# Attention's step loop with the normalisation behind two reductions, the splits of v one step on, their sums two steps behind, and early work placed anew

## The chip, the cores and the metric

The kernel runs on one core of one Trainium2 chip. The metric is the device time of one execution in microseconds (us). TensorE is called PE, and its weight loads, which run beside its matmuls, PEld; VectorE is DVE, ScalarE is ACT, GpSimd is POOL, and SyncE, on which nearly all DMAs are issued, is SP.

## The reference

Three stages follow each other. The first is attention over 2 batches of 8 heads, 768 rows of 64 each, with a mask: a score counts only where the signs of six random projections of q and of k are the same.

```python
mask = q_bucket[:, :, :, None] == k_bucket[:, :, None, :]
scores = np.where(mask, scale * np.matmul(q, k.transpose(0, 1, 3, 2)), -1e9)
scores = scores - np.max(scores, axis=-1, keepdims=True)
attn = np.exp(scores)
attn = attn / (np.sum(attn, axis=-1, keepdims=True) + 1e-09)
x = np.matmul(attn, v)                    # 16 heads -> x [1536, 512]
logits = x @ w_gate + modality_bias[modality_id]   # 8 experts, argmax, softmax weight
out[mask] = gate_w[mask, None] * (np.maximum(x[mask] @ w1[e], 0.0) @ w2[e])   # 512 -> 1024 -> 512
h = out @ w_in                            # 512 -> 2048
result = (np.maximum(h, 0.0) + alpha * np.minimum(h, 0.0)) @ w_out
```

The second sends each row of x to the one expert with the largest logit; the third is a feed-forward net over all rows.

## The kernel before, in words

The change lies in attention alone, so only that stage is told. Its work is written as one loop over steps, `for s in range(96+LAG+2)`. A step handles one sixth of a head (128 of its 768 keys); head h has the steps 6h to 6h+5. No loop runs on the chip: the program is written out, and each engine has one queue, in the order in which the loop writes. What stands in a step is set by `ORDER`, a word in which each letter stands for one kind of work, and by the table `PLAN`, which says in which step the work goes that comes once per head or once per group of heads.

The kinds of work of a step, with their lines:

- **ST** (letters a and b, halves of 384 queries): two matmuls (L861, L862) give the scores in a PSUM buffer `st`, ACT takes the exponential (L863). The first matmul holds the mask's bits and the row maximum as extra rows of the tile `op`, so it waits for the DMA that puts the row maximum there (`op<-mr`, L838).
- **MAX** (m and n, the same halves): a matmul on the mask's bits (L829) into `mxp`, reduced by DVE to a row maximum (L830, 0.55 us). A unit is one sixth of a head; units run some steps ahead of ST. `PLAN["cap"]` lists how many units a step takes, and behind the list's end it is two; but no unit is taken further than ten steps ahead, so that the steady rate is one. `st` and `mxp` share five PSUM buffers.
- **POSTa, POSTb** at the end of a head's MAX: a reduction (L832), a transpose on PE (L835), two short DVE instructions (L837, L841), and the DMAs of the row (L838) and of flags (L842) on SP.
- **EL** (e): the exponential is split into two halves of 16 bits, Eh on ACT (L867) and El on POOL (L868; on DVE from step 87 on).
- **AV** (A, in odd steps, for two sixths at a time, `LAG`=4 steps behind ST): 36 matmuls (L876 to L878) into the one PSUM buffer `av`. With a head's last sixth come the six L882.
- **NORM** (N, in steps 6h+10): three DVE instructions (L888, L889, L890) read `av` and write a head's part of x. The next head's AV, in the step behind, overwrites `av` and so waits for L890. For heads 7 and 15 NORM also issues the DMA of x (L892), on SP.
- **vsplit** of head h: ACT scales v into a PSUM buffer of the tag `misc` (L755, letter V), DVE splits it into `vh` (L759) and `vl` (L760, letter o). **vtot**: twelve small matmuls (L766, L767) sum them, and DVE keeps the sum in `vt` (L768, L769), which L882 reads. `misc` has two buffers, shared with Z, POSTb and the router.
- **Z**: six matmuls for a head's bits (L802 to L804, three for each half), DVE thresholds them (L809), and two DMAs on SP put them into the tile `op` (L650, `op<-big`), which MAX reads.
- **Router**: transposes of x on PE (L182) with a copy on DVE (L185), logits (L196, L200), and from step 57 a chain of small DVE instructions, cut into pieces; `PLAN["first"]` lists the steps of the pieces, the ninth being the gate weights.

In a step behind the steps of the start, the order of the letters in `ORDER` is: ST's first half (a), ACT's part of vsplit (V), the DMAs kept from before (D), NORM (N), MAX's first half (m), ST's second half (b), MAX's second half (n), EL (e), then POSTa, DVE's part of vsplit, AV and the rest.

Of the kernel before, what the change touches and what calls it, by code (L numbers as in the profile page):

```python
# [34 lines left out]
PB = 1  # L35
LAGS = (0, 0)
HB = 3
ORDER = "aVDNmbnefopAL"
PM = 2
PLAN = dict(  # L40
    v0=(1, 3, 4), T3=(2, 2), Z3=(4, 5), T=(2, 4, 5, 7), Z=(8, 10), ld=0, am1=(4, 6, 8, 9), am=(4, 6, 8,
    10), sc=(13, 15), tot=3, tot0=6, sp=(-2, 4, 10, 18), cap=(3, 2, 0, 1), x=(1, 2, 7, 3), x3=(0, 1, 2, 2), x4=(9, 10, 13, 11), w1=(91, 92, 95, 96, 97, 98, 99, 100), ga=(87, 88, 90), vl=1, am0=(0, 0), Z2=(0, 1), x6=(0, 1, 6, 4), first=(57, 58, 59, 60, 66, 72, 75, 78, 83, 84, 85, 86),
)
NPRE = 3
NT = 22
# [458 lines left out]
def _program(base, tc, nc, q, k, v, proj, mod, w_gate, mbias, w1, w2, win, wout, alpha, out):  # L504
# [445 lines left out]
    for s in range(96+LAG+2):  # L950
        us=[u for u in range(nu,min(96,s+6+LA+1,nu+(PLAN["cap"][s] if s<len(PLAN["cap"]) else 2)))]; nu+=len(us)
        fs=dq[:]; dq.clear()
        for o in "aVDNbmnefopAL" if s==0 else ORDER:
            t=s-1-LAG
# [613 lines left out]
```

## Time and profile before

| what | us |
|---|---|
| median of 3 executions | 685.57 (683.86 to 687.6) |
| the profiled execution | 686.88 |
| its span, first to last instruction | 685.1 |
| PE busy | 656.4 |
| PEld busy | 556.2 |
| DVE busy | 446.7 |
| ACT busy | 315.3 |
| POOL busy | 236.0 |

The span is what the trace covers; 1.8 us of the profiled execution lie around it. Busy time is the sum of the times in which an engine executes. Attention takes the first 250 us or so, and PE is the busiest engine in it and behind it.

### The profile page before, as it was taken

What the parts mean: (1) busy time and instruction counts of PE and PEld (TensorE: products, weight loads), DVE (VectorE), ACT (ScalarE), POOL (GpSimd) and SP (SyncE); (2) the same over time, 40 slices, a digit from 0 to 9 for tenths busy, and PEclk for the clock granted to TensorE, in tenths of its full rate; (3) what the DMA queues carried; (4) which work ended last, traced back from release to release, by engine and by line L of the source; (5) the groups of instructions that cost most, each with busy time, mean ns of one, the idle gap of its engine ahead of it and who ended that gap; (6) DMA issues with size and microseconds to landing.
All of it is one profiled execution on the core that took longest, in us unless ns stands there. A gap on an engine that the chain in (4) does not pass through costs nothing.

```text
span 685.1 us, 12778 instructions
## 1 busy us (share of the span) xinstructions
PE 656.4 (96%) x4938; PEld 556.2 (81%) x4938; DVE 446.7 (65%) x927; ACT 315.3 (46%) x536; POOL 236.0 (34%) x211
## 2 busy tenths in 40 slices
PE   7789999999999988999999999999999999999995
PEld 6578898998788878898888987888888888888884
DVE  6887878788888778455735668999443444433332
ACT  5567788887787843033423256665211111111111
POOL 8767999987967501310000202040030000200002
PEclk9979999999999999999999999999999999999998
DMA  8466864866603139385320834441020000100001
GB/s 217 129 146 142 187 154 97 185 185 138 140 11 125 49 107 395 119 321 201 108 61 11 285 120 154 131 146 62 1 93 1 15 16 0 47 16 0 1 0 61
DMA packets 32859, 75.02 MB, mean 110 GB/s; under 512 B 7276, under 2 KB 7366, under 8 KB 32534
## 3 DMA queue, kind: packets, MB, share of 16 engines
q1 hardware_dynamic: 29700, 64.43, 33.0%
q0 software_dynamic: 2960, 9.70, 4.3%
q8 instruction: 39, 0.64, 0.4%
q14 instruction: 30, 0.25, 0.1%
q10 hardware_dynamic: 130, 0.00, 0.0%
HBM read 49.79 MB, written 14.68 MB: 94 GB/s over the span
## 4 chain that ended last, share of the span: by engine, by line
PE 54%; DVE 1%; ACT 1%; issue 1%; POOL 1%; ACTq 0%; POOLq 0%
PE o L1413 19%; PE h L1387 18%; PE y L1074 8%; PE g L1054 8%; PE tr L1257 1%; POOL out_dram L1430 1%; PE tr L1041 0%; DVE w L1232 0%; DVE op L1232 0%; ACT op L1230 0%; DVE gl L620 0%; ACT gf L1391 0%; ACT q L1392 0%; ACT w L1230 0%; DVE big L1197 0%
## 5 line engine op out<-in xcount | busy, mean ns | idle before, releaser
L868 POOL TENSOR_TENSOR El<-E,Eh 128x768 f16<-128x768 f32 x87 | 142.7, 1652 | 36.6 <-ACT Eh L867 22.7
L863 ACT ACTIVATE E<-st 128x384 f32<-128x384 f32 x192 | 89.2, 494 | 53.3 <-PE st L862 49.8
L830 DVE TENSOR_REDUCE mx<-mxp 128x1 f32<-128x384 f32 x192 | 97.6, 548 | 9.2 <-PE mxp L829 8.7
L617 ACT ACTIVATE gh<-gf 128x512 fp32r<-128x512 f32 x48 | 30.3, 631 | 142.7 <-PE o L1413 132.2
L867 ACT ACTIVATE Eh<-E 128x768 f16<-128x768 f32 x94 | 79.8, 849 | 0.0
L861 PE MATMUL st<-op 97*128 97x384 f32 x192 | 72.9, 380 | 1.6 <-DMA op<-mr 1.3
L829 PE MATMUL mxp<-op 76*128 76x384 f32 x192 | 65.9, 357 | 7.3 <-ACT E L863 2.5
L620 DVE TENSOR_TENSOR gl<-gf,gh 128x512 fp32r<-128x512 f32 x48 | 33.1, 690 | 59.2 <-ACT gh L617 57.2
L1430 POOL DMA_INDIRECT out_dram<-x,did x12 | 11.8, 984 | 167.8 <-DVE x L1427 89.1
L1387 PE MATMUL h<-big,op 128*128 128x512 f32 x256 | 67.9, 393 | 0.0
L862 PE MATMUL st<-op 128*128 128x384 f32 x192 | 65.8, 343 | 0.0
L1413 PE MATMUL o<-op,gh 128*128 128x512 f32 x192 | 64.2, 395 | 0.0
L1245 POOL DMA_INDIRECT yg<-ys,dpos x10 | 12.3, 1231 | 138.3 <-DVE x L1197 72.8
L876 PE MATMUL av<-vh,Eh 128*128 128x65 f16 x576 | 58.5, 196 | 1.3 <-DVE big L890 1.3
L876 PEld LDWEIGHTS <-Eh 128*128 128x128 f16 x576 | 52.5, 98 | 8.4 <-issue 6.2
L1074 PE MATMUL y<-op,hh 128*128 128x512 f32 x172 | 58.6, 399 | 0.0
L877 PE MATMUL av<-vl,Eh 128*128 128x64 f16 x576 | 58.0, 194 | 0.0
L878 PE MATMUL av<-vh,El 128*128 128x65 f16 x576 | 57.8, 195 | 0.0
L1387 PEld LDWEIGHTS h<-big,op 128*128 128x128 f32 x256 | 48.1, 188 | 10.9
L877 PEld LDWEIGHTS <-Eh 128*128 128x128 f16 x576 | 53.2, 99 | 0.0
L878 PEld LDWEIGHTS <-El 128*128 128x128 f16 x576 | 53.1, 98 | 0.0
L1395 DVE TENSOR_SCALAR gf<-h,al 128x512 f32<-128x512 f32 x33 | 24.8, 751 | 41.7 <-PE h L1387 41.7
(424 smaller groups left out, 1483.2 us busy)
## 6 DMA issues: line engine op xcount, KB each, us to landing
r<-in_moe_w_dram SPq DMA_DIRECT2D x14, 1024.0 KB
op<-B SPq DMA_DIRECT2D x32, 192.0 KB
op<-A SPq DMA_DIRECT2D x28, 192.0 KB
op<-A SPq DMA_DIRECT2D x13, 384.0 KB
ys<-zero SPq DMA_DIRECT2D x19, 256.0 KB
op<-in_moe_w_in_dram SPq DMA_DIRECT2D x4, 1024.0 KB
op<-in_moe_w_out_dram SPq DMA_DIRECT2D x4, 1024.0 KB
ys<-ysb SPq DMA_DIRECT2D x13, 256.0 KB
```

The source lines that it names most:

```text
L829: mm(p[:,0:384],t[0:76,2,c*128:(c+1)*128],t[0:76,1,a*384:a*384+384],start=True,stop=True)
L830: nc.vector.tensor_reduce(out=mx[h][:,c,a:a+1],in_=p[:,0:384],axis=AX.X,op=ALU.max)
L861: mm(p[:,0:384],t[0:97,1,js],t[0:97,2,qs],start=True,stop=False)
L863: nc.scalar.activation(E[s][0][:,qs],p[:,0:384],AF.Exp,scale=0.125)
L867: else: nc.scalar.activation(eh,e,AF.Copy)
L868: (nc.vector if s>=ELD else nc.gpsimd).tensor_tensor(out=el,in0=e,in1=eh,op=ALU.subtract)
L876: mm(a[:,c*65:c*65+65],eh[:,cs],VH[h//4%2][:,j,h%4,:],start=(j==0 and c==0),stop=False,skip_group_check=True)
L877: mm(a[:,c*65:c*65+64],eh[:,cs],VL[h//4%2][:,j,h%4,:],start=False,stop=False,skip_group_check=True)
L878: mm(a[:,c*65:c*65+65],el[:,cs],VH[h//4%2][:,j,h%4,:],start=False,stop=False,skip_group_check=True)
L1074: nc.tensor.matmul(yps[key][i], a[:, ts], w[:, c], start=(c == 0 and m == 0), stop=(c == 7 and m == 2))
L1387: nc.tensor.matmul(p, terms[t][0][:, kk, cs], terms[t][1][:, kk], start=(n == 0), stop=(n == 11))
L1413: nc.tensor.matmul(po[b][i], a[:, ts], w[:, c % 2], start=(c == 0 and n == 0), stop=(c == 15 and n == 2))
```

## The change

Five entries are edited. In `ORDER`, N goes from before m to behind n. In `PLAN`, the first half of head 3's Z goes from step 4 to step 5, where the second half is; `cap` gets a longer list; the steps `sp` of the splits of v go one on (for the fourth head of each four one back; head 0 keeps its own), and `tot`, the distance from a split to its sum, goes from 3 to 2; the ninth piece of the router's chain goes from step 83 to 82.

```diff
--- before.py
+++ after.py
@@ -35,11 +35,11 @@
 PB = 1
 LAGS = (0, 0)
 HB = 3
-ORDER = "aVDNmbnefopAL"
+ORDER = "aVDmbnNefopAL"
 PM = 2
 PLAN = dict(
-    v0=(1, 3, 4), T3=(2, 2), Z3=(4, 5), T=(2, 4, 5, 7), Z=(8, 10), ld=0, am1=(4, 6, 8, 9), am=(4, 6, 8,
-    10), sc=(13, 15), tot=3, tot0=6, sp=(-2, 4, 10, 18), cap=(3, 2, 0, 1), x=(1, 2, 7, 3), x3=(0, 1, 2, 2), x4=(9, 10, 13, 11), w1=(91, 92, 95, 96, 97, 98, 99, 100), ga=(87, 88, 90), vl=1, am0=(0, 0), Z2=(0, 1), x6=(0, 1, 6, 4), first=(57, 58, 59, 60, 66, 72, 75, 78, 83, 84, 85, 86),
+    v0=(1, 3, 4), T3=(2, 2), Z3=(5, 5), T=(2, 4, 5, 7), Z=(8, 10), ld=0, am1=(4, 6, 8, 9), am=(4, 6, 8,
+    10), sc=(13, 15), tot=2, tot0=6, sp=(-1, 5, 11, 17), cap=(3, 2, 0, 1, 0, 2, 2, 2, 0, 2, 1, 1, 1, 1, 0), x=(1, 2, 7, 3), x3=(0, 1, 2, 2), x4=(9, 10, 13, 11), w1=(91, 92, 95, 96, 97, 98, 99, 100), ga=(87, 88, 90), vl=1, am0=(0, 0), Z2=(0, 1), x6=(0, 1, 6, 4), first=(57, 58, 59, 60, 66, 72, 75, 78, 82, 84, 85, 86),
 )
 NPRE = 3
 NT = 22
```

What the table does to MAX units: units 12 and 13 go from step 4 to 5, 14 and 15 from 5 to 6, 16 from 6 to 7, 18 from 8 to 9, and 24 from 14 to 15. Steps 4, 8 and 14 have none then, and step 15 has two, 24 and 25. From step 16 on each step has the unit that it had. The splits of v leave the steps 6h+10 in which NORM runs and go one step on; for heads 3, 7, 11 and 15 they go from steps 18, 42, 66 and 90 to 17, 41, 65 and 89, and their sums from 21, 45, 69 and 93 to 19, 43, 67 and 91. The order on POOL and on SP is the same before and after.

The first place is PE in steps 4 and 5, from ST's first half in step 4 on (`st` and `mxp` as above; `op_139` is head 0's tile, `op_141` head 2's; `mt` is the row maximum). Before:

```order
L861 MATMUL st<-op_139 128x384
L862 MATMUL st<-op_139 128x384
L829 MATMUL mxp<-op_141 128x384 x2
L861 MATMUL st<-op_139 128x384
L862 MATMUL st<-op_139 128x384
L829 MATMUL mxp<-op_141 128x384 x2
L802 MATMUL misc<-A,pwh 24x384
L803 MATMUL misc<-B,pwh 24x384
L804 MATMUL misc<-A,pwl 24x384
L835 MATMUL misc<-ident,mt_182 6x128
L861 MATMUL st<-op_139 128x384
L862 MATMUL st<-op_139 128x384
```

After:

```order
L861 MATMUL st<-op_139 128x384
L862 MATMUL st<-op_139 128x384
L861 MATMUL st<-op_139 128x384
L862 MATMUL st<-op_139 128x384
L835 MATMUL misc<-ident,mt_182 6x128
L861 MATMUL st<-op_139 128x384
L862 MATMUL st<-op_139 128x384
L829 MATMUL mxp<-op_141 128x384 x2
L861 MATMUL st<-op_139 128x384
L862 MATMUL st<-op_139 128x384
```

The two MAX units of step 4, and the first half of Z (L802 to L804), no longer stand before the transpose L835; both come later.

The second place is DVE around steps 15 to 17 (`av` is AV's buffer, `big_72` the part of x; L185 is the router's copy of step 17). Before:

```order
L749 COPY sc<-misc 128x4
L888 TENSOR_SCALAR r<-av,sc 128x6
L889 RECIPROCAL r<-r 128x6
L890 TENSOR_TENSOR big_72<-av,r 128x6x64
L830 TENSOR_REDUCE mx<-mxp 128x1 x4
L185 COPY big_73<-misc 128x384
L830 TENSOR_REDUCE mx<-mxp 128x1 x2
L759 CAST vh_190<-misc 128x6x64
L760 TENSOR_TENSOR vl_192<-misc,vh_190 128x6x64
```

After:

```order
L749 COPY sc<-misc 128x4
L830 TENSOR_REDUCE mx<-mxp 128x1 x2
L888 TENSOR_SCALAR r<-av,sc 128x6
L889 RECIPROCAL r<-r 128x6
L890 TENSOR_TENSOR big_72<-av,r 128x6x64
L830 TENSOR_REDUCE mx<-mxp 128x1 x2
L759 CAST vh_190<-misc 128x6x64
L760 TENSOR_TENSOR vl_192<-misc,vh_190 128x6x64
```

NORM's three instructions went behind the two reductions of its step. The split of v stands one step earlier, before the router's copy, since this is a fourth head; behind NORM there is one unit of MAX, that of step 17, before the split.

The third place is DVE in steps 89 to 93 (El and Eh are EL's, L185 and L200 the router's, `r` and `op_49..` an expert's weights). Before:

```order
L868 TENSOR_TENSOR El<-E,Eh 128x768
L759 CAST vh_191<-misc 128x6x64
L760 TENSOR_TENSOR vl_193<-misc,vh_191 128x6x64
L868 TENSOR_TENSOR El<-E,Eh 128x768
L620 TENSOR_TENSOR op_4953<-r_4014,op_4952 128x512
L866 CAST Eh<-E 128x768
L868 TENSOR_TENSOR El<-E,Eh 128x768
L200 TENSOR_TENSOR lg<-misc,lg 128x24
L620 TENSOR_TENSOR op_4953<-r_4014,op_4952 128x512
L868 TENSOR_TENSOR El<-E,Eh 128x768
L768 CAST vt<-misc 33x64
L769 TENSOR_TENSOR vt<-misc,vt 1x64
```

After:

```order
L868 TENSOR_TENSOR El<-E,Eh 128x768
L759 CAST vh_191<-misc 128x6x64
L760 TENSOR_TENSOR vl_193<-misc,vh_191 128x6x64
L185 COPY big_4016<-misc 128x384
L868 TENSOR_TENSOR El<-E,Eh 128x768 x2
L768 CAST vt<-misc 33x64
L769 TENSOR_TENSOR vt<-misc,vt 1x64
L620 TENSOR_TENSOR op_4968<-r_4014,op_4967 128x512
L866 CAST Eh<-E 128x768
L868 TENSOR_TENSOR El<-E,Eh 128x768
L200 TENSOR_TENSOR lg<-misc,lg 128x24
L620 TENSOR_TENSOR op_4968<-r_4014,op_4967 128x512
```

The split of head 15 (L759, L760) went ahead of a router copy and an El, and the sum's L768 and L769 ahead of two splits of weights, a cast, two El and a router addition.

## Rows read from the trace of the kernel before

**Rows 1.** The page: busy time, granted clock in 40 slices, end chain by line.
```profile
PE 656.4 (96%) x4938; PEld 556.2 (81%) x4938; DVE 446.7 (65%) x927; ACT 315.3 (46%) x536; POOL 236.0 (34%) x211
...
PEclk9979999999999999999999999999999999999998
...
PE o L1413 19%; PE h L1387 18%; PE y L1074 8%; PE g L1054 8%; PE tr L1257 1%; POOL out_dram L1430 1%; PE tr L1041 0%; DVE w L1232 0%; DVE op L1232 0%; ACT op L1230 0%; DVE gl L620 0%; ACT gf L1391 0%; ACT q L1392 0%; ACT w L1230 0%; DVE big L1197 0%
```

**Rows 2.** Windows of steps 4 and 5: length, busy per engine, clock, DMA, GB/s.
```profile
32.23:38.11 5.88, 4.24 (x15) 2.78 (x14) 4.10 (x11) 3.06 (x6) 4.29 (x3) 0.50 0.79 181
38.11:42.50 4.39, 4.39 (x40) 4.08 (x41) 3.30 (x8) 1.71 (x3) 2.94 (x3) 0.51 0.18 39
```

**Rows 3.** Timeline of PE, steps 4 to 6: start, length, instruction, idle before.
```profile
31.98 0.40 PE L747 MATMUL misc<-dg,one 128*128 128x4 f32 x2 [1.54 <-DVE dg L743]
...
33.88 0.98 PE L829 MATMUL mxp<-op 76*128 76x384 f32 x2 [0.66 <-ACT E L863]
...
38.08 0.37 PE L835 MATMUL misc<-ident,mt 128*6 128x128 f32 x1 [0.98 <-DVE vl L760]
...
43.18 0.34 PE L861 MATMUL st<-op 97*128 97x384 f32 x1
```

**Rows 4.** Timeline of PE, waits of steps 8, 13, 24, 58 and 60.
```profile
48.28 0.41 PE L829 MATMUL mxp<-op 76*128 76x384 f32 x1 [0.83 <-ACT A L711]
...
63.09 0.41 PE L829 MATMUL mxp<-op 76*128 76x384 f32 x1 [1.26 <-DMA op<-big]
...
85.85 0.45 PE L861 MATMUL st<-op 97*128 97x384 f32 x1 [0.71 <-DMA op<-mr]
...
161.56 0.35 PE L802 MATMUL misc<-A,pwh 128*48 128x384 f32 x1 [0.60 <-DVE r L888]
...
165.77 0.41 PE L861 MATMUL st<-op 97*128 97x384 f32 x1 [0.54 <-DMA op<-mr]
```

**Rows 5.** Timeline of SP's DMA issues: head 3's bits, two rows mr, x_d.
```profile
44.07 1.61 SPq L650 DMA_DIRECT2D op<-big  x2
...
80.61 0.76 SPq L838 DMA_DIRECT2D op<-mr  x1
...
146.94 0.35 SPq L892 DMA_DIRECT2D x_d<-big  x1
...
160.70 0.76 SPq L838 DMA_DIRECT2D op<-mr  x1
```

**Rows 6.** Timeline of PE and DVE, steps 16 and 17.
```profile
66.77 0.43 PE L861 MATMUL st<-op 97*128 97x384 f32 x1
...
67.73 0.34 PE L829 MATMUL mxp<-op 76*128 76x384 f32 x1
...
69.11 0.21 PE L876 MATMUL av<-vh,Eh 128*128 128x65 f16 x1
...
67.02 0.21 DVE L888 TENSOR_SCALAR r<-av,sc 128x6 f32<-128x6 f32 x1
...
67.50 0.56 DVE L890 TENSOR_TENSOR big<-av,r 128x384 f32<-128x384 f32 x1
67.97 1.94 DVE L830 TENSOR_REDUCE mx<-mxp 128x1 f32<-128x384 f32 x4
```

**Rows 7.** Timeline of DVE and PE, step 52.
```profile
146.35 0.56 DVE L890 TENSOR_TENSOR big<-av,r 128x384 f32<-128x384 f32 x1
...
146.97 0.55 PE L182 MATMUL misc<-ident,big 128*128 128x128 f32 x3
```

**Rows 8.** Timeline of DVE and PE, steps 89 to 95.
```profile
233.51 0.96 DVE L868 TENSOR_TENSOR El<-E,Eh 128x768 f16<-128x768 f32 x1 [1.23 <-ACT E L863]
...
234.97 0.56 DVE L760 TENSOR_TENSOR vl<-misc,vh 128x384 f16<-128x384 f32 x1
...
240.90 0.56 DVE L890 TENSOR_TENSOR big<-av,r 128x384 f32<-128x384 f32 x1
...
241.52 0.20 PE L876 MATMUL av<-vh,Eh 128*128 128x65 f16 x1 [1.27 <-DVE big L890]
```


## The prediction

> **What bounds the kernel now.** I read the page first. PE is busy in 656.4 of 685.1 us, and the end chain runs through the experts and the net (L1413, L1387), which the change does not touch [rows 1]. So PE in attention is the path, and a microsecond counts when PE idles or runs at the lower clock there. The page's clock line is at full level in all slices but the third (and nearly so in the first two): 34 to 51 us. The windows of steps 4 and 5 show the granted clock at 0.50 and 0.51, that is 1.2 instead of 2.4 GHz, while the first of them has PE busy for only 4.24 of 5.88 us [rows 2]. Then I read PE's timeline there. Ahead of L747 PE idles 1.54 us; at the lower clock it idles 0.66 us before unit 12 of MAX and 0.98 us before the transpose L835; from 38.08 on it has no gap, and step 6 begins at 43.18 [rows 3]. The later idle times are short and each has a name [rows 4]. Last I read what stands behind those names on SP and DVE [rows 5 to 8].
>
> All sums are made against the profiled execution, 686.88 us (span 685.1 and 1.8 around it), which lies 1.3 us above the median of 685.57; I subtract that at the end. What a measurement of this kernel can tell from no change is about 0.5%, 3.4 us.
>
> **Steps 4 to 24: a gain.** The wait of 0.66 us is put down to an exponential, but by the program unit 12 also needs head 2's bits, which come by DMA at that time; one step later both are there. The 0.98 us is L835 waiting for a `misc` buffer: the split of head 0 holds one until L760, and the first half of Z takes the other. With Z gone from step 4, L835 has a free buffer. So both gaps go: 1.64 us. Four matmuls of MAX (units 12 and 13 out, 14 and 15 on to step 6) leave the stretch too; at the lower clock they take some 0.32 us each (0.98 for an overlapping pair [rows 3]), later some 0.18 us at full clock. That gives 4 x (0.32 - 0.18) = 0.56 us. Together step 6 has a gain of 2.2 us, the clock lasting as long as now. If the clock is back before AV of step 5, which lies mostly in the low stretch now, its matmuls save about another 1 us: 3.3 us. The cause of the lower clock is the idle PE ahead of L747, which stays; what ended it in the trace was a PE without gaps since 38.08, and after the change PE has work without those gaps from 32.23 on.
>
> The Trainium skill, TensorE: Matmul & The Clock Gate, Part 1, says that the throttled state is the default and that activity of PE releases it. The trace agrees: the granted clock rose behind a stretch without gaps [rows 2, 3]. By that rule the gain would be the larger of the two figures.
>
> Behind this, unit 18 waits 0.83 us for head 3's bits [rows 4], whose DMA was issued at 44.07 [rows 5]; it comes a step later and its Z earlier, so that wait goes. The 1.26 us of unit 24 shrinks by 0 to 0.6. That would be 3.0 to 4.8 us. SP sets a limit: from 44.07 on it issues DMA behind DMA, until the row `mr` of head 4 goes out at 80.61, for which PE waits 0.71 us at step 24 [rows 4, 5]. So at step 24 PE can be earlier only by as much as SP's chain began earlier: the issue at 44.07 moves with Z's end, by 2.9 to 3.9 us. I take **-3.5** (bounds -1.6, the two gaps alone, and -4.5). The loss of step 17, below, is hidden here, since PE would wait at step 24 anyway.
>
> **NORM behind two reductions: a loss.** In step 16 NORM runs from 67.02 to 68.06, the reductions behind it (the four of 1.94 us are two for step 16, two for step 17), and AV's first matmul comes at 69.11 [rows 6]. After the change the first reduction starts at about 67.58, when its matmul is through; the second, whose matmul starts at 67.73 and takes 0.34, ends at 68.66; NORM adds 1.04 us and ends at 69.70. AV, which overwrites `av`, then starts 0.6 us later. What queues behind AV on PE is the whole next step. PE's queue has no other work to put there. This holds for the NORM steps without Z, where AV comes 2.3 to 2.6 us behind the step's start and NORM would end at 2.9: steps 16, 28, 40, 64, 82 (76 has 3.5 already). In those with Z (10, 22, 34, 46, 58, 70) AV comes at 3.2 us or later: nothing. So: step 17 hidden as said, 29 0.5, 41 0.6, 77 0.1, 83 0.5, and 65 nothing to 0.4, as PE waits for ACT in the steps around it; I take nothing. Sum **+1.7**. Below: nothing, if the reductions' earlier end frees `mxp` buffers sooner; above: 2.5.
>
> Step 52 is worse. The router's transposes L182 read the x that NORM of head 7 just wrote: L890 from 146.35 to 146.91, L182 at 146.97 [rows 7]. There NORM would end at about 148.7, so L182 and all of PE behind it is 1.7 us late. The DMA of x, issued at 146.94 between full transfers, is late by the same, and with it everything on SP up to the row `mr` issued at 160.70 [rows 5], for which step 60 waits already (0.54 us) [rows 4]. Step 58 gains its 0.60 us (Z waited for a `misc` buffer behind the split, which is gone from that step), but PE then only waits longer at 60. I take **+1.7**, bounds 1.0 and 1.8.
>
> **The splits and sums.** They are the same instructions, some 1.1 us of DVE for a split, moved to odd steps, which have AV on PE and DVE time to spare. Cover is AV's length, about 1.1 us for two sixths at full clock; without it, a split would delay the next reduction by 1.1 us. I cost it at nothing. Only at the end does it matter. In steps 89 to 95 DVE is the limit (it has El there too): it idles 1.23 us until 233.51, then has the split, till 235.53, and from there on hardly idles up to NORM of head 14, whose L890 at 240.90 ends the 1.27 us for which AV waits [rows 8]. Moved one step earlier, the split fills that hole, and NORM comes 1.1 us earlier: **-1.1** (bounds 0 and -1.6). The gate weights' piece, seven small instructions of DVE, moves into step 82 behind NORM: nothing, covered by AV of step 83, at most 0.5.
>
> **Sum.** -3.5 + 1.7 + 1.7 - 1.1 = -1.2: 686.88 becomes 685.7; against the median 684.4.
>
> **The rivals.** (1) *NORM's delay is not seen.* If AV is not there when NORM ends (its exponentials late, or PE a buffer behind), the +1.7 and most of step 52's go: -4.6 with nothing, so 681.0, with the gain at 4.5 680.0. For it: in six of the NORM steps AV comes late enough. Against: in step 16 AV came 1.05 us behind NORM's end and with no idle time before it [rows 6]. (2) *No early gain.* The two gaps go but other work, the rows on SP or unit 24's bits, takes the place: 1.7 + 1.7 - 1.1 = +2.3, so 687.9. For it: SP is full from 44.07 to 81 [rows 5]. Against: the first issue in that chain moves. (3) *Slower: the clock falls again at step 52.* The wait of 1.7 us there is longer than the 1.54 us that stands before the low stretch of step 4 [rows 3]. If the clock falls and stays low for as long as it did (32.23 to 42.50, 10.3 us, [rows 2]), dense work loses half of that, 5.1 us: 689.5. It decides from about 4.6 us on. Against: waits of 1.26 and 1.27 us [rows 4, 8] left the clock at full level [rows 1].
>
> The Trainium skill's same page, A second HAM failure mode, tells of a kernel in which many short idle times between groups of matmuls made the clock swing. That speaks for rival 3; in this trace the later short waits did not do so.
>
> **How the numbers follow.** The forecast gets 0.52, with a range of its own of 682.5 to 687 from its bounds; rival 1 0.2, rival 2 0.17, rival 3 0.11. Of the 8 in 10, the low end takes in most of rival 1 (680.8), the high end rival 2 and the edge of rival 3 (688.8). Faster by over 0.5% means under 682.1: nearly all of rival 1 and some of the forecast, 0.25; slower means over 689.0: 0.12, rival 3 and the ends of rival 2; within, 0.63.
>
> **What would show it.** Right: no idle time before L829 and L835 in steps 4 and 5, step 6 at 39 to 40.5; AV of steps 29, 41 and 83 with 0.5 us of idle time put down to L890; L182 of step 52 with 1.7; the row of step 24 landing 3 to 4 us earlier; AV at 241 waiting little. Wrong: the low clock elsewhere or longer than now, idle time before AV absent, SP's chain not earlier, or a new wait in steps 5 to 15, above all of unit 18 or 24.

## The result, and the profile after

The changed kernel takes 689.95 us in the median of 7 executions (688.6 to 691.16), the kernel before 685.88 (7 executions, 683.86 to 687.6). The ratio is 1.0063, 95% interval 1.0046 to 1.0081: slower by 3.2 to 5.6 us. The forecast was 684.4 us, and "slower" had a chance of 0.12. The profiled execution of the changed kernel takes 689.41 us, its span is 687.6.

The page first; its lines are those of [rows 1], engines' busy time and the granted clock in 40 slices.

```profile
PE 654.8 (95%) x4938; PEld 556.8 (81%) x4938; DVE 447.1 (65%) x927; ACT 316.2 (46%) x536; POOL 236.6 (34%) x211
...
PEclk9999999999999999999999999999999999999999
```

PE is busy for 1.6 us less than before and the span is 2.5 us longer, so PE is idle for 4.1 us more. (Busy time also holds what a low clock adds: before, a low stretch of some 10 us stands at 32 to 42 us; in its place are two short ones here, told below.) The list of what PE waited for (engine, line, releaser: sum, times, longest) names the idle time.

```profile
PE av L876 <- DVE big L890: 4.7, 7, 1.2
...
PE misc L182 <- DVE big L890: 2.0, 2, 1.8
...
PE st L861 <- DMA op<-mr: 1.4, 1, 1.4
PE misc L835 <- DVE mt L832: 1.4, 1, 1.4
```

Before, AV waited once for L890, 1.27 us [rows 8]; now seven times, 4.7 us in all. L182, the router's transposes, adds 2.0 us.

To see where the lag grows, I took from PE's timelines the start of ST in each step, and compared the distance from step 3 (the times ahead of step 3 differ by up to 1.5 us from execution to execution of like code, and are left out). Minus is earlier than before:

| at step | changed kernel against before, us |
|---|---|
| 5 | -4.90 |
| 6 | -3.04 |
| 10 | -1.39 |
| 16 | -1.45 |
| 18 | +0.01 |
| 24 | -0.81 |
| 40 | -0.36 |
| 52 | +0.15 |
| 53 | +2.03 |
| 55 | +3.60 |
| 60 | +2.57 |
| 84 | +3.77 |
| 95 | +3.62 |

From step 24 to 95 the changed kernel takes 157.88 us, before 153.45: 4.4 us lost. Up to 24 it gained 0.8, not 3.5.

**Steps 4 to 16.** PE's timeline, to be read against [rows 3, 4]:

```profile
31.02 0.39 PE L747 MATMUL misc<-dg,one 128*128 128x4 f32 x2 [1.54 <-DVE dg L743]
...
35.17 0.44 PE L829 MATMUL mxp<-op 76*128 76x384 f32 x1 [1.13 <-ACT E L863]
...
39.18 0.42 PE L861 MATMUL st<-op 97*128 97x384 f32 x1 [1.43 <-DMA op<-mr]
...
46.03 0.27 PE L835 MATMUL misc<-ident,mt 128*6 128x128 f32 x1 [1.40 <-DVE mt L832]
...
62.35 0.44 PE L829 MATMUL mxp<-op 76*128 76x384 f32 x1 [1.15 <-ACT E L863]
```

The gaps of 0.66 and 0.98 us are gone, as forecast. In their place are 1.13 us ahead of the last unit of step 5, 1.43 us at step 6, for the DMA of head 1's row of maxima, 1.40 us ahead of the transpose of step 8, and 1.15 us in step 15. That is 5.1 us where the four waits that went had 3.7. The two waits put down to an exponential are waits for a free PSUM buffer: L829 reads nothing that ACT makes, and a step with two units of MAX takes six buffers of the five that `st` and `mxp` share, two for ST and four for MAX. So the sixth has to wait until one of the step's own has been read. In both steps the trace says by whom: by ACT, which reads ST's first half. ACT's timeline of steps 5 and 15:

```profile
33.90 0.84 ACT L711 ACTIVATE A<-big 128x768 fp32r<-128x768 f32 x1
34.63 0.87 ACT L863 ACTIVATE E<-st 128x384 f32<-128x384 f32 x2
...
61.07 0.84 ACT L711 ACTIVATE A<-big 128x768 fp32r<-128x768 f32 x1
61.80 0.87 ACT L863 ACTIVATE E<-st 128x384 f32<-128x384 f32 x2
```

One exponential takes 0.49 us, so the first of each pair ends at 35.12 and 62.29, and PE's matmul follows at 35.17 and 62.35. Ahead of the pair ACT makes the copy A of a later head's operand, 0.84 us. Step 15 has two units only since the change. Step 5 had two before, but now begins 1.0 us behind step 4, so that ACT is behind.

The wait of step 8 is DVE's:

```profile
42.80 1.95 DVE L830 TENSOR_REDUCE mx<-mxp 128x1 f32<-128x384 f32 x4
```

Step 7 too has two units only since the change. Its four reductions, and the split of v behind them, hold L832 up, for which L835 waits in step 8.

The row for step 6 stands in SP's queue behind five DMAs of head 2's operands, three of A from 31.36 on and two of B:

```profile
34.32 1.53 SPq L650 DMA_DIRECT2D op<-B  x2
35.95 0.77 SPq L838 DMA_DIRECT2D op<-mr  x1
...
39.59 1.61 SPq L650 DMA_DIRECT2D op<-big  x2
...
77.49 0.76 SPq L838 DMA_DIRECT2D op<-mr  x1
```

Before, the row for step 6 was issued here, 4.0 us ahead of the step, and PE did not wait for it:

```profile
39.19 0.77 SPq L838 DMA_DIRECT2D op<-mr  x1
```

So, counted from step 3, the row goes out 2.3 us earlier, while step 5 begins 4.9 us earlier.

Against [rows 5], head 3's bits go out 4.5 us earlier and the row of head 4 3.1 us earlier, of which 1.0 us lies ahead of step 3. PE has no wait for that row at step 24 any more, so SP's chain behind head 3's bits was not what took the gain.

The windows of steps 4 and 5 had a clock of 0.50 and 0.51 [rows 2]. Now (from, to, length, busy times, clock, DMA share, GB/s):

```profile
32.25:39.18 6.93, 4.31 (x52) 2.94 (x52) 5.07 (x11) 3.98 (x8) 6.93 (x5) 1.00 0.75 172
64.36:68.00 3.64, 3.64 (x14) 3.58 (x13) 2.04 (x6) 2.20 (x5) 2.33 (x3) 0.53 0.59 111
148.00:152.00 4.00, 3.93 (x49) 3.80 (x50) 3.03 (x6) 2.84 (x5) 3.26 (x4) 0.72 0.82 344
152.00:156.00 4.00, 4.00 (x26) 3.85 (x26) 2.76 (x7) 2.19 (x5) 3.77 (x3) 0.85 0.98 247
```

The early stretch runs at full clock, although the wait of 1.54 us ahead of L747 is still there. But a low one stands at 64 to 68 us, behind the wait of step 15, and another behind step 52.

**NORM.** Step 28, with the same instructions as step 16 in [rows 6] and at full clock:

```profile
92.37 1.09 DVE L830 TENSOR_REDUCE mx<-mxp 128x1 f32<-128x384 f32 x2 [1.42 <-PE mxp L829]
...
93.96 0.56 DVE L890 TENSOR_TENSOR big<-av,r 128x384 f32<-128x384 f32 x1
...
94.58 0.20 PE L876 MATMUL av<-vh,Eh 128*128 128x65 f16 x1 [0.65 <-DVE big L890]
```

NORM begins behind the two reductions, ends at 94.52, and AV waits 0.65 us for it. In step 52, against [rows 7]:

```profile
147.37 0.56 DVE L890 TENSOR_TENSOR big<-av,r 128x384 f32<-128x384 f32 x1
...
148.07 0.52 PE L182 MATMUL misc<-ident,big 128*128 128x128 f32 x3 [1.80 <-DVE big L890]
```

L182 waits 1.80 us. Behind it the clock is at 0.72 and 0.85, and the lag goes from +0.15 to +3.60 us within three steps.

**The end.** Steps 89 to 95, against [rows 8]:

```profile
232.32 0.58 ACT L755 ACTIVATE misc<-vr,sc 128x384 f32<-128x384 f32 x1
...
233.06 0.55 DVE L185 COPY big<-misc 128x384 f32<-128x384 f32 x1
...
235.61 0.56 DVE L760 TENSOR_TENSOR vl<-misc,vh 128x384 f16<-128x384 f32 x1
...
243.46 0.56 DVE L890 TENSOR_TENSOR big<-av,r 128x384 f32<-128x384 f32 x1
...
233.66 0.55 PE L182 MATMUL misc<-ident,big 128*128 128x128 f32 x3 [0.37 <-DVE big L185]
...
244.08 0.20 PE L876 MATMUL av<-vh,Eh 128*128 128x65 f16 x1 [1.17 <-DVE big L890]
```

The split does fill DVE's hole. But from 232.32 on it also holds one of the two `misc` buffers, so the transposes of step 89 (L182 at 233.66) wait 0.37 us for the other, until L185 at 233.06 has copied those of step 88. Before, the same transposes had a buffer at once:

```profile
230.33 0.52 PE L182 MATMUL misc<-ident,big 128*128 128x128 f32 x3
```

Counted from step 88, NORM's L890 comes only 0.24 us earlier than before, and AV in step 95 still waits 1.17 us.

### The profile page after: what moved, and what is told of

It is laid out like the page before. It is cut to its first block, busy times and chain, and to the rows that moved or that the text cites. A ratio compares the mean times of both kernels' runs of the same rounds, so it can differ in the third digit from the quotient of the medians.

```text
span 687.6 us, 12772 instructions
## 1 busy us (share of the span) xinstructions
PE 654.8 (95%) x4938; PEld 556.8 (81%) x4938; DVE 447.1 (65%) x927; ACT 316.2 (46%) x536; POOL 236.6 (34%) x211
## 4 chain that ended last, share of the span: by engine, by line
PE 54%; DVE 1%; ACT 1%; issue 1%; POOL 1%; ACTq 0%; POOLq 0%
PE o L1413 19%; PE h L1387 18%; PE y L1074 8%; PE g L1054 8%; PE tr L1257 1%; POOL out_dram L1430 1%; PE tr L1041 0%; DVE w L1232 0%; DVE op L1232 0%; ACT op L1230 0%; DVE gl L620 0%; ACT gf L1391 0%; ACT q L1392 0%; ACT w L1230 0%; DVE big L1197 0%
## 5 line engine op out<-in xcount | busy, mean ns | idle before, releaser
L829 PE MATMUL mxp<-op 76*128 76x384 f32 x192 | 65.1, 356 | 5.9 <-ACT E L863 3.1
```

## The experiments

The kernel before was timed beside each; ratios are to it. Diffs show the edit to the kernel named.

**All but NORM.** The changed kernel, with:

```diff
-ORDER = "aVDmbnNefopAL"
+ORDER = "aVDNmbnefopAL"
```

> The changed kernel with the old ORDER: NORM ahead of the reductions again, all else as changed. Theory A (the loss is NORM's later end: 0.5 to 0.8 us at each of steps 17, 29, 41, 65, 77, 83 and, at step 52, a wait of 1.8 us and a low clock behind it, 3.4 us in all): 1 to 2 us faster than the kernel before, about 684.5, and no idle time of PE put down to L890 in steps 17 to 83 except the 0.2 us of step 52. Theory B (the loss is in the early units of MAX and the splits of v): 2 us or more slower than before, about 688 to 690.

Measured: 685.43 us, ratio 0.9992 (0.9976 to 1.0009). The waits for L890 in its list:

```profile
PE av L876 <- DVE big L890: 1.2, 1, 1.2
...
PE tr L182 <- DVE big L890: 0.6, 1, 0.6
...
PE misc L182 <- DVE big L890: 0.2, 1, 0.2
```

One wait of AV is left, that of step 95, and 0.2 us of L182. Theory B falls: with the early units and the splits in place the loss is gone. The gain of 1 to 2 us that theory A wanted is not there either (-0.5 us, interval -1.6 to +0.6).

**NORM alone.** The kernel before, with the opposite edit.

> The kernel before with the new ORDER alone. Theory A: 4 to 5 us slower than before, about 690, with the waits for L890 of the changed kernel at the same steps, longer where the split of v still stands in the step. Theory B: within 1.5 us of before.

Measured: 691.05 us, ratio 1.0079 (1.0058 to 1.0101), 5.4 us slower. Its step 52, PE's timeline and the window behind:

```profile
148.36 0.55 PE L182 MATMUL misc<-ident,big 128*128 128x128 f32 x3 [1.71 <-DVE big L890]
```

```profile
148.00:152.00 4.00, 3.64 (x36) 3.34 (x37) 3.26 (x7) 2.23 (x5) 3.16 (x4) 0.62 0.74 310
```

The order alone gives more than the whole loss, by the same wait and the same fall of the clock.

**The early part alone.** The kernel before, with `Z3=(5, 5)` and the new `cap`.

> The kernel before with the new cap and the first half of head 3's Z in step 5 alone. Theory A: the early part is worth what the changed kernel's trace shows up to step 24, some 0.8 us faster (0.5 us slower to 2 us faster), with a new wait of about 1.4 us at step 6 for the DMA of head 1's row. Theory B: 2 us slower.

Measured: 684.67 us, ratio 0.9986 (0.9973 to 0.9999), 1.0 us faster, as theory A said. In its profiled execution the gain is 2.2 us at step 24 and stays at 2.2 up to step 95. It had a low clock in step 5 (step 6 begins at 39.85):

```profile
31.00:39.00 8.00, 7.14 (x54) 5.60 (x55) 5.34 (x15) 5.26 (x10) 8.00 (x6) 0.61 0.70 157
39.00:43.00 4.00, 4.00 (x33) 3.38 (x30) 3.62 (x8) 2.36 (x5) 1.40 (x2) 0.93 0.42 110
```

so PE came to step 6 late and the wait for the row did not show there. So the wait of about 1.4 us that was expected at step 6 is not in this trace.

Among the nine profiled executions with the early part, three pictures appear. At full clock, with the wait of 1.4 us, step 6 begins 3.0 us earlier than before (two). With a low clock in step 5 alone and no wait it begins 2.8 to 2.9 us earlier (two). With the clock low up to 40 to 42 us, about as long as before, and no wait, it begins 2.1 us earlier (five).

The gain is in part, perhaps wholly, the clock's: the mean granted clock of the 12 executions is 0.9888, that of the 29 of the kernel before beside them 0.9867, which over 685 us is an estimated 1.4 us of full speed, uncertain by some 0.7.

**The splits alone.** The kernel before, with `tot=2`, the new `sp`, and 82 for 83 in `first`.

> The kernel before with the new steps of the splits, the shorter distance to the sums and the ninth router piece in step 82 alone. Theory A: within 1 us of before; at the end, PE waits for the router's copy in step 89 what it no longer waits for NORM in step 95. Theory B: 1 to 2 us slower.

Measured: 686.71 us, ratio 1.0011 (0.9996 to 1.0026), no change that shows. At the end, PE's timeline has

```profile
231.21 0.55 PE L182 MATMUL misc<-ident,big 128*128 128x128 f32 x3 [0.37 <-DVE big L185]
```

and the lag grows by 0.94 us from step 88 to 92 and falls by 1.07 from 92 to 95. That is an exchange, but not quite the one expected: AV in step 95 still waits 1.18 us. Of the two sums some 0.4 us each are the matmuls of the sum of v, which stand in step 91 and no longer in step 93; and L196 of step 94 no longer has its 0.45 us of waiting for DVE's L200. Ahead of that, this trace gains 0.8 us from step 60 to 76, loses 0.5 in step 77 and 1.5 behind it, where the clock is low (0.57 from 205 to 209 us).

**NORM early in step 52 alone.** The changed kernel, with:

```diff
-        for o in "aVDNbmnefopAL" if s==0 else ORDER:
+        for o in "aVDNbmnefopAL" if s==0 else "aVDNmbnefopAL" if s==52 else ORDER:
```

> The changed kernel with NORM ahead of the reductions in step 52 alone. Theory A1 (of NORM's later end, step 52 is the largest part: 1.8 us of waiting and 1.6 us of low clock behind it, of which about 1 us comes back at steps 58 and 60): 2.4 to 3.4 us faster than the changed kernel, 686.5 to 687.5; no wait of 1.8 us at L182 and the clock at full level from 148 to 156 us. Theory A2 (the small waits for L890 ahead of AV make it up, step 52 is absorbed by later waits): within 1 us of the changed kernel, 689 to 690.

Measured: 687.24 us, ratio 1.0015 (0.9999 to 1.0031), which is 3.3 us less than the changed kernel's ratio gives (some 1.7 to 4.9, an estimate from the two intervals). The window behind step 52:

```profile
148.00:152.00 4.00, 4.00 (x48) 4.00 (x45) 3.68 (x11) 3.44 (x7) 4.00 (x5) 1.00 0.99 329
152.00:156.00 4.00, 4.00 (x65) 3.44 (x63) 3.06 (x8) 3.10 (x6) 4.00 (x3) 1.00 0.97 240
```

**NORM late in step 52 alone.** The kernel before, with "aVDmbnNefopAL" for step 52 in the same line.

> The kernel before with NORM behind the reductions in step 52 alone. A1: 2.4 to 3.4 us slower than before, 688.5 to 689.3, with the wait at L182 and a granted clock under 1 behind it. A2: within 1 us of before.

Measured: 688.35 us, ratio 1.0038 (1.0023 to 1.0054), 2.6 us slower. So by the medians one step of 102 makes up more than half of the loss, from either side; the low end of this interval, 1.6 us, is less than half. Its profiled execution has the wait and not the fall of the clock:

```profile
147.54 0.55 PE L182 MATMUL misc<-ident,big 128*128 128x128 f32 x3 [1.71 <-DVE big L890]
```

```profile
148.00:152.00 4.00, 4.00 (x58) 3.85 (x57) 3.76 (x8) 3.37 (x7) 3.74 (x5) 1.00 0.96 393
```

**The router's transposes one step later.** The changed kernel, with:

```diff
-x3=(0, 1, 2, 2)
+x3=(1, 2, 3, 3)
```

> The changed kernel with the router's transposes of steps 52 and 53, and the logits of step 54, each one step later; NORM stays late everywhere. If the transposes L182 are what waits for NORM in step 52: the 1.8 us shrink to the 0.5 or 0.6 us for which AV waits in step 53, the clock does not fall there, and the time is 2 to 3 us below the changed kernel, 687 to 688. If it is the DMA of x, issued late, that holds up the row for step 60: as the changed kernel, 689.5 to 690.5.

Measured: 689.38 us, ratio 1.0048 (1.0031 to 1.0064): about 1 us less than the changed kernel by the ratios, which is within their intervals. The 2 to 3 us of the first case are not there in the medians. The 1.8 us are gone and the clock is at 1.00 there, but at step 60 PE waits anew, for a row that SP issued late:

```profile
167.83 0.41 PE L861 MATMUL st<-op 97*128 97x384 f32 x1 [1.58 <-DMA op<-mr]
```

```profile
149.08 0.35 SPq L892 DMA_DIRECT2D x_d<-big  x1
...
162.84 0.76 SPq L838 DMA_DIRECT2D op<-mr  x1
```

From step 52 to 60 this kernel loses 1.75 us, the changed one 2.42. Most of the wait taken away at L182 is met again behind the DMA of x.

**And x's DMA behind that row.** The kernel just told, with:

```diff
-            nc.sync.dma_start(out=x_d[...], in_=xs[b])
+            def out(): nc.sync.dma_start(out=x_d[...], in_=xs[b])
+            if b: out()
+            else: at(57, out)
```

> The kernel with the router's transposes one step later (changed otherwise), in which the DMA of x for the first batch is issued in step 57, behind the row that step 60 waits for, instead of at the end of NORM in step 52. If that DMA, late with NORM, holds up SP's queue and so the row: no wait of 1.6 us at step 60, and 1.5 to 2 us below the kernel with the transposes moved alone, 687.4 to 687.9. If the transfers behind it are the limit by themselves, wherever x goes: within 0.7 us of that kernel, 689.4, or slower, if the router's first piece then waits for the x buffer.

Measured: 689.06 us, ratio 1.0053 (1.0033 to 1.0072). SP's timeline has the row at 159.59, with x behind it:

```profile
159.59 0.75 SPq L838 DMA_DIRECT2D op<-mr  x1
```

In the trace step 60 has no wait and nothing is lost from step 52 to 60 (0.00 us in place of 1.75). The medians do not show that gain: 689.06 lies in the range of the second case, and the intervals of the two kernels overlap by more than the gain. So that x's DMA holds up the row is shown in the trace; what it is worth over many executions stays open.

**Head 1's row on ACT's queue.** The early part alone, with:

```diff
-        nc.sync.dma_start(out=f32(OP[h%NP][96:97,2,...
+        (nc.scalar if h==1 else nc.sync).dma_start(out=f32(OP[h%NP][96:97,2,...
```

> The kernel with the early part alone (cap and Z), and head 1's row of maxima issued on ACT's queue instead of SP's, where five DMAs of head 2 stand ahead of it. If SP's queue is what takes the early gain back at step 6: step 6 begins about 1.4 us earlier, the SP issues behind it 0.9 us earlier, and the time is about 0.9 us below the early part alone, 683.8. If it is the transfer itself or the bunched reductions: no gain, 684.7.

Measured: 684.59 us, ratio 0.9986 (0.9973 to 1.0), no gain over the early part alone. The row goes out at 35.30 with no DMA ahead of it, but the execution has the low clock in step 5, and ST of step 6 starts at 39.99, no earlier:

```profile
35.30 0.79 ACTq L838 DMA_DIRECT2D op<-mr  x1
...
35.98 0.69 PE L829 MATMUL mxp<-op 76*128 76x384 f32 x1 [0.55 <-DVE mx L830]
...
39.99 0.34 PE L861 MATMUL st<-op 97*128 97x384 f32 x1
```

The edit is not a clean one: the issue stands on ACT's queue ahead of step 5's exponentials, which start at 36.19 here and at 35.16 in the early part alone. So this does not settle the row's price at full clock. The wait of step 5, for a free buffer as above, is here put down to a reduction on DVE, so which reader frees a buffer in time differs with the edit.

**cap cut short.** The early part alone, with:

```diff
-cap=(3, 2, 0, 1, 0, 2, 2, 2, 0, 2, 1, 1, 1, 1, 0)
+cap=(3, 2, 0, 1, 0, 2, 2, 2)
```

> The kernel with the early part alone, but cap cut behind its eighth entry, so that unit 18 stays in step 8 and unit 24 in step 14 as before (steps 9 and 15 have one unit). If the two units in step 15 give back what the wait for head 4's bits gave (four reductions in a row, PE 1.15 us without a free buffer), and the bits are there by now in step 14: 0.8 to 1.5 us below the early part alone, 683.2 to 683.9. If the bits are the limit wherever unit 24 stands: PE waits about 1.2 us in step 14, and the time is as before the cut, 684.7.

Measured: 684.84 us, ratio 0.9979 (0.9964 to 0.9993), 1.4 us faster than before and the best of all, but not to be told from the early part alone. The 1.15 us of step 15 are gone, with 0.34 us in their place:

```profile
62.94 0.45 PE L861 MATMUL st<-op 97*128 97x384 f32 x1 [0.34 <-DVE mx L830]
```

The wait went as in the first case expected, the time did not: 684.84 is what the second case gave. From step 10 to 16 this kernel gains 0.6 us in its trace and the early part alone 0.1; from 16 to 24 they gain 0.6 and 0.9. So about half of what unit 24 gave was taken back by step 24. The rest was lost ahead of step 10, with the clock low up to 42 us.

**NORM between the halves.** The changed kernel, with:

```diff
-ORDER = "aVDmbnNefopAL"
+ORDER = "aVDmNbnefopAL"
```

> The changed kernel with NORM between the two halves' reductions (one 0.55 us reduction ahead of it, not two). If each reduction ahead of NORM delays it by its own length and PE pays what exceeds the slack: the waits of 0.6 us ahead of AV fall to 0.1 or less, that of step 52 from 1.8 to about 1.2 us, and the time is 2 to 3 us below the changed kernel, 687 to 688. If it is the order as such (a wait that exists or not): as the changed kernel, 690.

Measured: 686.97 us, ratio 1.0015 (1.0003 to 1.0027), 3.3 us below the changed kernel. Step 52:

```profile
148.31 0.53 PE L182 MATMUL misc<-ident,big 128*128 128x128 f32 x3 [1.27 <-DVE big L890]
```

1.27 us in place of 1.80, and only one other wait of AV, of 0.5 us, besides that of step 95. Each reduction ahead of NORM delays it by its own 0.55 us, and PE pays what exceeds the slack.

## Why the prediction was wrong

- **"Steps 4 to 24: a gain", -3.5.** The two gaps went and step 5 began 4.9 us earlier, as argued. The step that failed is the next: I followed the waits that go, but not what is late next. Units put off meet in pairs in later steps, where they take six buffers of five and put four reductions in a row on DVE; and head 1's row, which step 6 reads, went out only 2.3 us earlier. PE waited anew in steps 5, 6, 8 and 15, 5.1 us in all. Ahead of step 8, where no unit is owed any more, the executions with the early part are 1.9 to 2.2 us ahead, or 0.9 to 1.0 where the clock stayed low up to 40 to 42 us; the forecast had 3.3 and 2.2. Measured: -0.8 at step 24 in the changed kernel's trace, -1.0 us (-1.9 to -0.1) for the part alone. The limit by SP, on which the -3.5 rested, was not the one that acted. The cause given for the low clock, the idle time ahead of L747, is not enough either: it stands in the changed kernel's trace too, and the clock is full there.
- **Unit 18: "that wait goes".** The 0.83 us went, and 1.40 us came in the same step, for DVE's L832. (The row names ACT's copy for the 0.83, not the bits; in the trace of NORM alone the wait there, 0.66 us, is for the bits' DMA.)
- **Unit 24: "shrinks by 0 to 0.6".** It changed its cause, not its size: 1.26 us for the bits before, 1.15 us for a buffer now. With the unit back in step 14 (which is where the 1.26 us stood; [rows 4] has it as step 13) PE waited 0.34.
- **"NORM behind two reductions", +1.7 for AV.** The mechanism and the size of one wait were right: 0.6 forecast, 0.55 to 0.65 measured at steps 29, 41 and 83. The sum was too small by three places taken at nothing or little: 0.97 us in step 77 (0.1), 0.54 in step 65 (nothing), 0.26 in step 59 (nothing, and the only one in a step with Z: its wait for `misc` had gone, so AV came earlier). All but step 95: 3.5 us. The wait ahead of 17 was hidden by about half, not wholly. In the changed kernel the clock fell there too, but the run with NORM early in step 52 alone has that wait (0.55 us) at full clock: against the run with all but NORM it loses 0.56 us from step 16 to 18, and 0.25 of that is left at step 24.
- **Step 52, +1.7.** The wait was 1.80 us, as worked out, and it was not swallowed at step 60. Alone it is worth 2.6 us (late in the kernel before) and 3.3 us (early in the changed one). The excess is in part the clock behind it: rival 3, which I gave 0.11, happened in the changed kernel's trace and in that of NORM alone, at a price of some 1.6 us there (the lag from step 53 to 55), not 5.1; part came back at steps 58 and 60. The ground against it, that waits of 1.26 and 1.27 us left the clock at full level, held for that one execution: behind the like wait of step 95 the clock fell in six of thirteen. Over many executions the excess fits: the mean granted clock is 0.9871 in the changed kernel and 0.9888 with NORM early in step 52, 0.9867 in the kernel before and 0.9852 with NORM late in that step, an estimated 1.0 to 1.2 us each time, uncertain by some 0.7. The loss of the whole kernel is not a lower clock, though, since the changed kernel's mean is no lower than that of the kernel before.
- **The splits, nothing, and the end, -1.1.** The splits cost nothing that shows (+0.7 us, -0.3 to +1.8, with the end in it). The -1.1 failed: I read DVE's hole as the cause of the wait in step 95, so that NORM would come as much earlier as the split did. It came 0.24 us earlier, and the wait fell from 1.27 to 1.17. Nor did I ask what else the split holds: the second `misc` buffer, for which the router's transposes then wait. Measured +0.9 us in steps 88 to 92 and -1.1 behind.
- **The sum.** The parts alone give -1.0 + 5.4 + 0.7 = +5.1 us, the whole +4.3 (1.0063). Two terms were mis-sized, the early gain by 2.5 us and NORM by 2.0, both in the same direction; the term at the end, 1.1, was an exchange.

What stays open: why the clock falls in one execution and not in another with the same wait, the worth of x's DMA, and what head 1's row costs at full clock.

## What to carry to other kernels

Before an instruction goes behind others on an in-order engine, list what waits for its result on the bottleneck, and take its slack in every step, not in a typical one: here a step in which the router reads the result at once cost more than half of the loss. When work is deferred to close a gap, count the buffers of the step in which it lands, and look at the engines that free them: two units in one step took six buffers of five here, and PE paid what ACT and DVE were behind. Work that fills a hole on a busy engine takes its buffers along: look who else needs them.

## What was unexpected of the hardware

A wait of PE of 1.7 to 1.8 us at step 52 was followed by a low granted clock in two of the three profiled executions that have it at L182 (0.72 and 0.62 in the 4 us window from 148; 1.00 in the third), and one of 1.27 us in the one with NORM between the halves was not. But shorter waits were followed by one elsewhere. AV in step 95 waits 1.15 to 1.28 us in all thirteen profiled executions, and six of them have a low stretch at that wait or right behind it:

```profile
240.00:244.00 4.00, 3.52 (x50) 3.51 (x51) 3.97 (x7) 1.65 (x3) 0.00 (x0) 0.57 0.00 0
```

That is the run with all but NORM; in the kernel before and the changed one this stretch is at 1.00. So it can't be said from these traces how long a wait the clock bears.

The low stretch that the kernel before has at 32 to 42 us is absent there from the changed kernel, which has one at 64 to 68. The kernel with the router's transposes moved alone is like it (1.00 up to 62 us, 0.75 and 0.50 in the two windows from 62 to 70). All others with the early part, which run nearly the same instructions there, have the low stretch early (0.61 from 31 to 39 in the early part alone). So the same code has its low stretch in different places, and single profiles differ by 1 us or so in their early steps.
